# A state-space layer and a GELU layer on one core: the first four chunks of tokens brought in as rows of four, and the order of all steps written as a list

## The chip, the cores and the metric

The kernel runs on one core of a Trainium2 chip. The metric is the device time in microseconds of one execution; three executions of the kernel before were timed, and a fourth execution was profiled. The engines are called PE (TensorE, with its weight loads as PEld), DVE (VectorE), ACT (ScalarE), POOL (GpSimd) and SP (SyncE, which issues nearly all transfers).

## The reference

Four batches of 768 tokens with eight heads pass through a scan with decaying state, and the result through a two-layer network with a tanh GELU. Cut to what matters:

```python
# x: (4, 8, 768, 32)   a: (4, 8, 768)   B, C: (4, 8, 768, 16)
log_a = np.log(np.clip(a, 1e-6, 1.0))
for c in range(S // 32):                      # chunks of the reference
    cum = np.cumsum(la, axis=-1)
    L = np.exp(cum[..., :, None] - cum[..., None, :]) * causal
    y = einsum(C, B) * L @ x  +  (C @ state) * exp(cum)
    state = exp(sum(la)) * state + sum_j B_j x_j exp(cum[-1] - cum_j)
h = y.transpose(0, 2, 1, 3).reshape(3072, 256) @ w_in       # 256 x 2048
out = gelu_tanh(h) @ w_out                                  # 2048 x 256
```

The kernel takes and gives fp32 and multiplies in bf16.

## The kernel before

**Tiling.** The kernel works on chunks of Q = 128 tokens, 24 in all (NCH), six for each batch (CPB). `UNITS` groups them: chunk 0 alone, chunk 1 alone, then eleven pairs. The eight heads lie side by side, so that B and C of a chunk are 128 x 128 (heads times 16 states) and x is 128 x 256.

**Decays.** Instead of exponentials of sums, a scan (`f_R`) multiplies the decays backward from the end of each chunk, `f_RT` and `f_RT0` turn the result to one token per partition with fp32 products, and B is multiplied by it and C by its reciprocal (`f_mul`, `f_mul0`). `f_pe`, `f_pp` and `f_pend` make one decay per chunk, spread over the partitions.

**Attention of a unit.** The scaled B and C are transposed (`f_T`, `f_T0`), evicted (`f_E`, `f_bh0`, `f_ce0`, `f_F`; C twice, masked for even and odd heads), and B is transposed back (`f_N`, `f_bn`). Then, for each unit: `f_G` makes the 128 x 128 products of B and C of all heads, `f_M` masks them to the causal triangle on DVE, `f_D` makes the contribution to the state, `f_S` adds it to the decayed state, `f_SP` spreads the state for the next chunk, `f_Y` adds both parts of y in PSUM, and `f_yev` evicts y, already transposed, to `xm`.

**The two layers.** `f_s1` multiplies a group of the first layer, four products of 128 x 128 weights with 256 tokens, into one of two PSUM buffers (pool `psh`), `f_gelu` evicts it, `f_s2` multiplies four of the 16 parts of the second layer, `f_oev` evicts 128 tokens and `f_store` stores them.

**Weights.** `w_in` and `w_out` come in four pieces each (`load_wi`, `load_wo`, 512 KB) into six buffers and are cast to bf16 (`f_wi`, `f_wo`), mostly on POOL. The cast of `w_in` also reorders the columns, so that columns k, k+4, k+8 and so on of a piece become adjacent, to suit the order in which `w_out` is loaded.

**Loads.** x is loaded one chunk at a time with a token on each partition, which makes pieces of 128 bytes; B and C of chunk 0 likewise, in pieces of 64 bytes; B and C of a batch with six tokens on each partition, in pieces of 384 bytes. All but two go through SP's queue.

**Order.** Every step is a `Node` with an engine, a duration, dependencies, a priority and the buffers that it takes. `run_order` walks through them in time and writes down an order, which is also the order of issue on each engine. Where PE would be idle early on, `idle` puts in products of zeros (77 fillers, L776), which nobody reads.

Of the kernel before, what the change touches and what calls it, by code (L numbers as in the profile page):

```python
# [8 lines left out]
FP32 = mybir.dt.float32  # L9
BF16 = mybir.dt.bfloat16  # L10
AF = mybir.ActivationFunctionType
ALU = mybir.AluOpType

# [17 lines left out]
def run_order(nodes, pools, hop=0.08, same=0.04, idle=None, wait=()):  # L31
# [6 lines left out]
    def est(n):  # L38
        t = 0.0
        for d in n.deps:  # L40
            if d.end is None:
                return None
            t = max(t, d.end + n.after
                    + (d.done + hop if d.eng != n.eng else 0.0 if n.eng == "PE" else same))
        for pool, _ in n.allocs:
            h = hist[pool]
            if len(h) >= pools[pool]:
                for d in h[-pools[pool]]:
                    if d.end is None:
                        return None  # L50
                    t = max(t, d.end + (same if d.eng == n.eng else hop))
        return t
# [41 lines left out]
def kernel(  # L94
# [10 lines left out]
    nc = tc.nc  # L105
# [4 lines left out]
    CPB = S // Q  # L110
    R6 = CPB
    NCH = batch * CPB
    HC = CPB // 2
    HS = S // 2
    d_ff = moe_w_in.shape[1]
# [3 lines left out]
    UNITS = [[0], [1]] + [[c, c + 1] for c in range(2, NCH, 2)]  # L119
    NU = len(UNITS)  # L120

    const = ctx.enter_context(tc.tile_pool(name="const", bufs=1))
    ld = ctx.enter_context(tc.tile_pool(name="ld", bufs=batch))
    wfp = ctx.enter_context(tc.tile_pool(name="wfp", bufs=6))
    ldx = ctx.enter_context(tc.tile_pool(name="ldx", bufs=NU))
# [13 lines left out]

    a_t = const.tile([64, HS], FP32, name="a_t")  # L140
    a_half = [bass.AP(tensor=a.tensor, offset=a.offset + i * HS, ap=[[S, batch * H], [1, HS]])
              for i in range(2)]
    XF, X16 = {}, {}
    U = [dict() for _ in range(batch)]
    bc0 = const.tile([128, 2, H, N], FP32, name="bc0")

    def load_bc0(i, q):
        q.dma_start(out=bc0[:, i], in_=(B, C)[i][0, :, 0:Q, :].rearrange("h p n -> p h n"))

    def load_bc(b, i):  # L150
        d = U[b]
        if "bc" not in d:
# [4 lines left out]
    nc.sync.dma_start(out=a_t[0:32], in_=a_half[0])  # L157
    nc.scalar.dma_start(out=a_t[32:64], in_=a_half[1])
    load_bc0(1, nc.sync)
    load_bc0(0, nc.scalar)  # L160

    wz = const.tile([128, 512], BF16, name="wz")
    nc.vector.memset(wz, 0.0)
    warm = const.tile([128, 1], FP32, name="warm")
    nc.vector.memset(warm, 0.0)  # L165
    nc.scalar.activation(warm, warm, AF.Gelu_apprx_tanh)
    ends = const.tile([64, Q], FP32, name="ends")
    nc.vector.memset(ends, 0.0)
    nc.vector.memset(ends[:, Q - 1:Q], 1.0)
    ac = const.tile([64, HS + 1], FP32, name="ac")  # L170
    nc.vector.memset(ac[:, HS:HS + 1], 0.0)
    pe1 = const.tile([64, HC], FP32, name="pe1")
    pe2 = const.tile([64, 2 * batch, HC], FP32, name="pe2")

    idf = const.tile([64, 64], FP32, name="idf")
    nc.gpsimd.memset(idf, 0.0)
    nc.gpsimd.affine_select(out=idf, in_=idf, pattern=[[-1, 64]], compare_op=ALU.not_equal,
                            fill=1.0, base=0, channel_multiplier=1)
    ident = const.tile([128, 128], BF16, name="ident")
    make_identity(nc, ident)  # L180
    bmask = const.tile([128, H * D], BF16, name="bmask")
    nc.gpsimd.memset(bmask, 1.0)
    bm3 = bmask.rearrange("p (h d) -> p h d", h=H)
    nc.gpsimd.affine_select(out=bm3, in_=bm3, pattern=[[-N, H], [0, D]],
                            compare_op=ALU.is_ge, fill=0.0, base=0, channel_multiplier=1)
    nc.gpsimd.affine_select(out=bm3, in_=bm3, pattern=[[N, H], [0, D]],
                            compare_op=ALU.is_ge, fill=0.0, base=N - 1, channel_multiplier=-1)
    tri = const.tile([128, Q], BF16, name="tri")
    make_upper_triangular(nc, tri, val=1.0, diag=True)
    tri_b = tri.rearrange("p (o q t) -> p o q t", o=1, q=1).to_broadcast([128, 4, 2, Q])  # L190

    sel8 = const.tile([64, H], FP32, name="sel8")
    nc.vector.tensor_reduce(out=sel8, in_=idf.rearrange("p (b h) -> p h b", h=H),
                            op=ALU.add, axis=mybir.AxisListType.X)
    selp = const.tile([64, H, N], FP32, name="selp")
    nc.vector.tensor_copy(out=selp, in_=sel8.rearrange("p (h o) -> p h o", o=1)
                          .to_broadcast([64, H, N]))
    m8 = const.tile([64, 2 * batch], FP32, name="m8")
    nc.gpsimd.memset(m8, 1.0)
    nc.gpsimd.affine_select(out=m8, in_=m8, pattern=[[-H, 2 * batch]], compare_op=ALU.is_ge,  # L200
                            fill=0.0, base=0, channel_multiplier=1)
    nc.gpsimd.affine_select(out=m8, in_=m8, pattern=[[H, 2 * batch]], compare_op=ALU.is_ge,
                            fill=0.0, base=H - 1, channel_multiplier=-1)
    par = const.tile([128, 2], FP32, name="par")
    bmp = bmask.rearrange("p (g e d) -> p e g d", g=4, e=2)
    for e in range(2):
        nc.vector.tensor_reduce(out=par[:, e:e + 1],
                                in_=bmp[:, e, :, 0:1].rearrange("p g o -> p (g o)"),
                                op=ALU.add, axis=mybir.AxisListType.X)
    r_t = const.tile([64, HS], FP32, name="r_t")  # L210

    rt = const.tile([128, R6, batch * H], FP32, name="rt")
    pt = const.tile([128, R6, batch * H], FP32, name="pt")
    q0 = const.tile([128, H], FP32, name="q0")
    bc0s = const.tile([128, 2, H, N], BF16, name="bc0s")
    ce0 = const.tile([128, 2, Q], BF16, name="ce0")
    bh0 = const.tile([128, Q], BF16, name="bh0")
    pend = const.tile([128, NCH], FP32, name="pend")
    WF = {}
    w_in_sb = const.tile([128, 2, d_ff], BF16, name="w_in_sb")  # L220
    w_out_sb = const.tile([128, NF, d_model], BF16, name="w_out_sb")
    xm = const.tile([128, 2, n_tokens], BF16, name="xm")


    gb = ps1.tile([128, 4, 512], FP32, name="gb")
    yb = ps1.tile([128, 512], FP32, name="yb")
    y4 = yb.rearrange("p (c w t) -> p c w t", c=2, w=2)
    rp0 = yb[:, 0:H]
    T6 = [gb[:, 2 * i, 0:S // 2].bitcast(BF16) for i in range(2)]
    T6_0 = [yb[:, 0:S // 2].bitcast(BF16), T6[1]]  # L230

    T0, DT, MT, RP = {}, {}, {}, {}
    state = {}
    gts, ops, hps, outs = {}, {}, {}, {}

    def load_x(u):
        b, c = divmod(UNITS[u][0], CPB)
        XF[u] = ldx.tile([128, 2, H, D], FP32, name="x_t")
        for k in range(len(UNITS[u])):
            nc.sync.dma_start(out=XF[u][:, k], in_=x[b, :, (c + k) * Q:(c + k + 1) * Q, :]  # L240
                              .rearrange("h p d -> p h d"))

# [10 lines left out]

    def copy(eng, o, i):
# [7 lines left out]
    def f_wi(q, k0, k1, eng):  # L262
        for k in range(k0, k1):
            copy(eng, w_in_sb[:, k, q * 512:(q + 1) * 512].rearrange("d (k p) -> d k p", k=4),
                 WF[("i", q)][:, k].rearrange("d (p k) -> d k p", k=4))

    def f_wo(q, eng):
        copy(eng, w_out_sb[:, 4 * q:4 * q + 4], WF[("o", q)])


    def f_clip(i0, i1):
        nc.vector.tensor_scalar(out=ac[:, i0:i1], in0=a_t[:, i0:i1], scalar1=1e-6, scalar2=1.0,
                                op0=ALU.max, op1=ALU.min)
# [7 lines left out]
    def f_RT0():  # L281
        nc.tensor.matmul(out=rp0, lhsT=r_t[0:32, 0:Q], rhs=idf[0:32, 0:H], start=True, stop=True,
                         skip_group_check=True)

    def f_RT(r0, r1):
        if r0 == 0:
            RP[1] = psh.tile([128, 512], FP32, name="hp")[:, 0:R6 * batch * H] \
                .rearrange("p (r j) -> p r j", r=R6)
        r6 = r_t.rearrange("q (p r) -> q r p", r=R6)
        for r in range(r0, r1):  # L290
# [6 lines left out]
    def f_recip0():  # L297
        nc.vector.reciprocal(q0, rp0)

# [3 lines left out]
    def f_recip(b0, b1):  # L303
        js = slice(b0 * H, b1 * H)
        nc.vector.reciprocal(pt[:, :, js], (rt if b0 else RP[1])[:, :, js])
# [17 lines left out]


    def f_mul0(i):
        nc.vector.tensor_tensor(
            out=bc0s[:, i], in0=bc0[:, i],
            in1=(rp0, q0)[i].rearrange("p (h o) -> p h o", o=1).to_broadcast([128, H, N]),
            op=ALU.mult)

    def f_T0(i):
        T0[i] = psh.tile([128, 512], FP32, name="hp").bitcast(BF16)[:, 0:Q]
        nc.tensor.transpose(out=T0[i], in_=bc0s[:, i].rearrange("p h n -> p (h n)"), identity=ident)

    def f_ce0():
        for e in range(2):
            nc.vector.tensor_scalar(out=ce0[:, e], in0=T0[1], scalar1=par[:, e:e + 1],
                                    scalar2=None, op0=ALU.mult)

    def f_bh0():  # L340
# [472 lines left out]
```

## Time and profile before

| | |
|---|---|
| three timed runs | 124.19, 124.71 and 126.72 us, median 124.71 |
| profiled execution | span 122.8 us, 3507 instructions; the page gives no total of its own beside the span |
| PE | 114.6 us busy (93%), 1506 products, of them 77 fillers |
| DVE, ACT, POOL | 68.3, 74.9, 23.0 us busy |
| last product, last eviction, end | PE ends at 119.1, DVE's last eviction takes 0.42 us, the span ends at 122.8 |
| transfers | 14.09 MB in 40591 packets, 35904 of them under 512 bytes |

PE's busy time counts fillers and products at half clock like any other, and products overlap, so a busy PE need not be doing useful work at its full rate. A row of a group reads: line, engine, operation, output and input, sizes, how many; then busy time, mean duration of one, and the idle time of the engine before them. A row of windows reads: the stretch, its length, the busy time of PE, PEld, DVE, ACT and POOL with the number of instructions, the granted clock of PE (1.00 is full), the share of the DMA engines and the GB/s that they moved.

### The profile page before, as it was taken

Reading aid. Unit: us, or ns where it says so; the run is one execution under the profiler, and the core shown is the slowest. Engines: PE = TensorE matmul, PEld = TensorE weight load, DVE = VectorE, ACT = ScalarE, POOL = GpSimd, SP = SyncE. Lnnn points to the kernel's source line nnn. Section 1 sums busy time; section 2 is a strip of 40 time slices with the busy share of each in tenths; the row PEclk is TensorE's granted clock in tenths of the full one; section 3 lists DMA queues with packets and bytes.
Section 4 is the critical chain, followed back from the end, with each engine's and each line's share of the span. In section 5 each row is a group of like instructions: output and inputs, shape, how many; then the busy total and the mean of one; then the engine's idle time right before and its main releaser. Section 6 shows DMA issues by size and latency. Waiting matters only on the chain.

```text
span 122.8 us, 3507 instructions
## 1 busy us (share of the span) xinstructions
PE 114.6 (93%) x1506; PEld 96.2 (78%) x1506; DVE 68.3 (56%) x116; ACT 74.9 (61%) x145; POOL 23.0 (19%) x38
## 2 busy tenths in 40 slices
PE   5899978989799999999999999999999999999970
PEld 5687747778678798787879889787878888888860
DVE  3897999968849888184979672475663000000110
ACT  4025536674676677656686777865768766786310
POOL 7206967750320160122000000000000000000000
PEclk9975699999999999999999999999999999999999
DMA  3999959989799899851101101101110111100121
GB/s 52 242 266 265 328 112 370 320 191 200 128 229 221 127 235 216 145 134 48 43 0 48 43 0 48 43 0 48 43 43 5 45 43 45 45 21 22 43 90 43
DMA packets 40591, 14.09 MB, mean 115 GB/s; under 512 B 35904, under 2 KB 39040, under 8 KB 40576
## 3 DMA queue, kind: packets, MB, share of 16 engines
q1 hardware_dynamic: 39488, 13.75, 46.4%
q8 instruction: 12, 0.20, 0.7%
q10 hardware_dynamic: 1088, 0.11, 0.7%
q14 instruction: 3, 0.02, 0.1%
HBM read 10.72 MB, written 3.15 MB: 113 GB/s over the span
## 4 chain that ended last, share of the span: by engine, by line
PE 70%; SPq 18%; DMA 5%; DVE 3%; issue 1%; DVEq 0%
PE o_ps L523 29%; PE hp L506 29%; SPq L240 7%; DMA bc_t<-in_B_dram 5%; SPq L252 5%; SPq L154 4%; PE yb L523 3%; SPq L248 3%; PE gb L408 2%; PE yb L451 2%; PE yb L460 2%; PE gb L358 2%; DVE ch L260 2%; PE gb L379 1%; DVE bc L349 1%
## 5 line engine op out<-in xcount | busy, mean ns | idle before, releaser
L514 ACT ACTIVATE gT<-hp 128x512 bf16<-128x512 f32 x96 | 53.6, 596 | 24.4 <-PE hp L506 24.2
L506 PE MATMUL hp<-xm,w_in_sb 128*128 128x256 bf16 (+1 forms) x416 | 53.7, 267 | 0.9 <-POOL w_in_sb L258 0.4
L523 PE MATMUL o_ps<-w_out_sb,gT 128*128 128x256 bf16 x352 | 47.3, 273 | 0.0
L506 PEld LDWEIGHTS <-w_in_sb 128*128 128x128 bf16 x416 | 37.6, 99 | 7.7 <-issue 2.0
L523 PEld LDWEIGHTS <-gT 128*128 128x128 bf16 x384 | 37.1, 98 | 4.8 <-issue 0.4
L418 DVE TENSOR_TENSOR m<-gb,tri 128x1024 bf16<-128x1024 f32 (+1 forms) x25 | 29.1, 1173 | 1.9 <-PE gb L408 1.8
L532 DVE COPY o_sb<-o_ps 128x256 f32<-128x256 f32 x2 | 0.8, 424 | 25.6 <-PE o_ps L523 25.6
L258 POOL CAST x<-x_t 128x512 bf16<-128x512 f32 (+1 forms) x12 | 8.5, 710 | 25.0 <-DMA x_t<-in_x_dram 20.1
L479 DVE SCALAR_TENSOR_TENSOR s_new<-s_new,pend,hp 128x64 f32<-128x64 f32 x16 | 4.5, 279 | 11.5 <-PE hp L429 11.2
L776 PE MATMUL o_ps<-wz 128*128 128x128 bf16 x77 | 8.9, 267 | 1.3 <-DVE warm L165 1.3
L530 ACT ACTIVATE o_sb<-o_ps 128x256 f32<-128x256 f32 x20 | 7.7, 385 | 3.8 <-PE o_ps L523 2.1
L486 DVE SCALAR_TENSOR_TENSOR sp_new<-s_new,pend,bmask 128x256 bf16<-128x256 f32 x20 | 10.0, 506 | 0.0
L469 ACT ACTIVATE xm<-yb 128x512 bf16<-128x512 f32 (+1 forms) x13 | 7.3, 564 | 4.3 <-PE yb L460 2.1
L258 POOL CAST w_in_sb<-wf 128x512 bf16<-128x512 f32 x6 | 7.0, 1193 | 7.0 <-DMA wf<-in_moe_w_in_dram 7.0
L776 PEld LDWEIGHTS <-wz 128*128 128x128 bf16 x77 | 6.5, 122 | 1.8 <-DVE warm L165 1.2
L460 PE MATMUL yb<-m,x 128*32 128x128 bf16 x192 | 6.3, 223 | 0.6 <-DVE m L418 0.6
L373 DVE TENSOR_SCALAR ce<-ch,par 128x768 bf16<-128x768 bf16 (+2 forms) x10 | 5.9, 634 | 0.8 <-ACT ch L256 0.8
L451 PE MATMUL yb<-ce,sp_new 128*32 128x128 bf16 x160 | 5.3, 221 | 0.0
L408 PE MATMUL gb<-ce,bh 32*128 32x256 bf16 x96 | 5.1, 278 | 0.0
L460 PEld LDWEIGHTS <-x 128*32 128x32 bf16 x192 | 3.8, 97 | 1.5 <-issue 1.5
L358 PEld LDWEIGHTS <-bc 128*128 128x128 bf16 x48 | 3.8, 110 | 1.3 <-issue 1.1
L258 POOL CAST w_out_sb<-wf 128x1024 bf16<-128x1024 f32 x4 | 4.4, 1112 | 1.5 <-DMA wf<-in_moe_w_out_dram 1.5
(72 smaller groups left out, 61.6 us busy)
## 6 DMA issues: line engine op xcount, KB each, us to landing
x_t<-in_x_dram SPq DMA_DIRECT2D x24, 128.0 KB, 4.5
out_dram<-o_sb SPq DMA_DIRECT2D x24, 128.0 KB, 1.7
wf<-in_moe_w_in_dram SPq DMA_DIRECT2D x4, 512.0 KB, 6.9
wf<-in_moe_w_out_dram SPq DMA_DIRECT2D x4, 512.0 KB, 6.0
bc_t<-in_C_dram SPq DMA_DIRECT2D x4, 384.0 KB, 4.4
bc_t<-in_B_dram SPq DMA_DIRECT2D x4, 384.0 KB, 5.4
bc<-in_B_dram ACTq DMA_DIRECT2D x1, 64.0 KB, 4.2
bc<-in_C_dram SPq DMA_DIRECT2D x1, 64.0 KB, 2.8
```

The lines of the kernel that those rows point to most:

```text
L240: nc.sync.dma_start(out=XF[u][:, k], in_=x[b, :, (c + k) * Q:(c + k + 1) * Q, :] .rearrange("h p d -> p h d"))
L258: nc.gpsimd.tensor_copy(out=o, in_=i)
L408: nc.tensor.matmul(out=gb[:, g, 256 * k:256 * k + 256], lhsT=bh_of(gc)[32 * g:32 * g + 32], rhs=ce_of(gc)[32 * g:32 * g + 32], start=True, ...
L418: nc.vector.tensor_tensor(out=MT[gc][:, g0:g1], in0=gb[:, g0:g1, 256 * k:256 * k + 256] .rearrange("p g (e t) -> p g e t", e=2), in1=tri_b ...
L451: nc.tensor.matmul(out=y4[32 * j:32 * j + 32, k, w], lhsT=sp[:, 32 * h:32 * h + 32], rhs=ce_of(gc)[:, h % 2], start=first(j), stop=False, ...
L460: nc.tensor.matmul(out=y4[32 * j:32 * j + 32, k, w], lhsT=X16[u][:, k, 32 * h:32 * h + 32], rhs=m[:, h // 2, h % 2, :], start=first(j), st ...
L486: nc.vector.scalar_tensor_tensor(out=sp_new.rearrange("p (g d) -> p g d", g=4), in0=state[("s", gc)].rearrange("p (o d) -> p o d", o=1).to ...
L506: nc.tensor.matmul(out=hp[:, j * nt:(j + 1) * nt], lhsT=w_in_sb[:, kc, fi * 128:(fi + 1) * 128], rhs=xm[:, kc, t0:t0 + nt], start=(kc == 0 ...
L514: nc.scalar.activation(gts[u][:, i * per:(i + 1) * per, 0:nt], hps.pop((u, i)).rearrange("p (j t) -> p j t", j=per), AF.Gelu_apprx_tanh)
L523: nc.tensor.matmul(out=ops[gc], lhsT=gts[u][:, fi, tt * Q:(tt + 1) * Q], rhs=w_out_sb[:, fi, :], start=(fi == 0), stop=(fi == NF - 1), ski ...
L530: nc.scalar.activation(o_sb, ops.pop(gc), AF.Copy)
L776: nc.tensor.matmul(out=zb[:, 0:128], lhsT=wz[:, 0:128], rhs=wz[:, 0:128], start=True, stop=True)
```

## The change

1. All twelve units are pairs of chunks.
2. B and C of chunks 0 to 3 are loaded together with four tokens on each partition (pieces of 256 bytes), those of chunks 4 and 5 with two. The decays of batch 0 come in a tile of their own (`a0_t`, 48 rows of 128), those of the other batches are worked out later (`decays`).
3. x of chunks 0 to 3 is loaded as rows of four tokens as well (pieces of 512 bytes). `f_XX` sets it to one token per partition with products by 0/1 matrices (`unp`); `f_XD` makes the state contributions of these four chunks straight from the rows.
4. The first pair's mask goes by quarters: `f_M0` does two of the four groups of heads on DVE, ACT evicts the other two (`f_GE`), and POOL and DVE mask one each (`f_M0s`). Its y is evicted in two halves, and its part of the second layer goes quarter by quarter, both chunks in turn.
5. `w_in` is cast without reordering, one half piece at a time; `f_s1` reads its weight columns four apart (`w_in_k`).
6. The order is a list of node numbers (`ORDERED`; A, D or P after a number moves the step to ACT, DVE or POOL; fN puts in N fillers, 47 in all). Evictions may now go to ACT or DVE.
7. Buffers: seven for weights, two instead of four for B and C of a batch, six for x.

The core of the diff:

```diff
-    UNITS = [[0], [1]] + [[c, c + 1] for c in range(2, NCH, 2)]
-    NU = len(UNITS)
+    NU = NCH // 2
+    GR = ((0, 4), (4, 2))
...
+    def load_bc0(g, i, q=None):
+        c, n = GR[g]
+        (q or nc.sync).dma_start(out=BC0[g][:, i],
+                                 in_=(B, C)[i][0, :, c * Q:(c + n) * Q, :]
+                                 .rearrange("h (p r) n -> p h (r n)", r=n))
...
+    def load_x4():
+        WF["x"] = wfp.tile([128, H, R4 * D], FP32, name="wf")
+        nc.sync.dma_start(out=WF["x"], in_=x[0, :, 0:R4 * Q, :].rearrange("h (p r) d -> p h (r d)", r=R4))
...
-    def f_wi(q, k0, k1, eng):
-        for k in range(k0, k1):
-            copy(eng, w_in_sb[:, k, q * 512:(q + 1) * 512].rearrange("d (k p) -> d k p", k=4),
-                 WF[("i", q)][:, k].rearrange("d (p k) -> d k p", k=4))
+    def f_wi(q, k, eng):
+        copy(eng, w_in_sb[:, k, q * 512:(q + 1) * 512], WF[("i", q)][:, k])
...
+    def f_RT0(g):
+        c0, n = GR[g]
+        m = Q // n
+        rr = r0_t.rearrange("q (p r) -> q r p", r=n)
+        for r in range(n):
+            for c in range(n):
+                nc.tensor.matmul(out=rp0[g][m * c:m * c + m, r], lhsT=rr[:, r],
+                                 rhs=id0[:, :, c0 + c], start=True, stop=True,
+                                 tile_position=(0, m * c), skip_group_check=True)
...
+    def f_XX(u):
+        for r in range(R4):
+            for k in range(2):
+                c = 2 * u + k
+                cs = slice(P4 * c, P4 * c + P4)
+                nc.tensor.matmul(out=XN[c][:, 0:H * D], lhsT=unp[cs, r].rearrange("p q s -> p (q s)"),
+                                 rhs=x4b[cs, :, r], start=(r == 0), stop=(r == R4 - 1),
+                                 tile_position=(P4 * c, 0), skip_group_check=True)
+
+    def f_XD(u):
...
+        for r in range(R4):
+            for g in range(4):
+                for k in range(2):
...
+                    nc.tensor.matmul(out=XN[c][32 * g:32 * g + 32, H * D:H * D + 64],
+                                     lhsT=bc0s[0][cs, 0, r, 2 * g:2 * g + 2].rearrange("p h n -> p (h n)"),
+                                     rhs=x4b[cs, 2 * g:2 * g + 2, r], start=(r == 0), stop=(r == R4 - 1),
+                                     tile_position=(P4 * c, 32 * g), skip_group_check=True)
...
     def f_s1(u, i):
...
+            q, k = divmod(2 * i + j, 4)
+            for w in range(2):
+                nc.tensor.matmul(out=hp[:, j * T:(j + 1) * T], lhsT=w_in_k[:, w, q, k],
+                                 rhs=xm[:, w, u * T:(u + 1) * T], start=(w == 0), stop=(w == 1))
...
-    for t, fn in run_order(nodes, pools, idle=idle, wait=("DVE", "POOL")):
-        fn()
+    for w in ORDERED.split():
+        if w[0] == "f":
+            fill(int(w[1:]))
+        else:
+            n = nodes[int(w.rstrip("ADP"))]
+            n.eng = {"A": "ACT", "D": "DVE", "P": "POOL"}.get(w[-1], n.eng)
+            n.fn()
```

In the new order PE runs, after the opening fillers: f_RT0 for both groups of chunks, the transposes of C and B of chunks 0 to 3, G of unit 0, f_pp0, XD(0), XX(0), G(1), Y(0), XD(1), XX(1), then the first s1 groups of unit 0 with Y(1), the first group of the second layer and the transposes of chunks 4 and 5 among them. SP issues the first `w_in` pieces after x, then the first `w_out` piece, the last `w_in` piece, B and C of chunks 4 and 5, the other `w_out` pieces, B and C of batch 1 and then x of the later pairs.

## The prediction

> **What bounds the kernel now.** I read the page first (slices, chain), then TensorE (PE) stage by stage, then its groups. The profiled execution has a span of 122.8 us; the three timed runs have a median of 124.71 us, so 1.9 us lie outside the span, and I keep them unchanged. On this kernel a measurement tells about 2% from no change: the cut for "faster" is 122.2 us.
>
> ```profile
> PEclk9975699999999999999999999999999999999999
> DMA  3999959989799899851101101101110111100121
> GB/s 52 242 266 265 328 112 370 320 191 200 128 229 221 127 235 216 145 134 48 43 0 48 43 0 48 43 0 48 43 43 5 45 43 45 45 21 22 43 90 43
> ...
> PE 70%; SPq 18%; DMA 5%; DVE 3%; issue 1%; DVEq 0%
> ```
>
> The chain ends on PE, and its first quarter is the SP queue and a load: two stages. DMA is full until about 40 us and nearly idle afterwards. The stages, from the table of windows:
>
> ```profile
> 0.00:13.60 13.60, 11.78 (x122) 9.52 (x123) 10.01 (x31) 4.78 (x12) 6.41 (x20) 0.79 0.91 223
> 13.60:31.74 18.14, 15.71 (x257) 12.40 (x258) 16.21 (x22) 10.68 (x20) 10.25 (x11) 0.97 0.95 238
> 31.74:119.10 87.36, 87.09 (x1128) 74.25 (x1127) 41.64 (x65) 59.43 (x115) 6.30 (x9) 1.00 0.33 76
> 119.10:122.80 3.70, 0.00 (x0) 0.00 (x0) 0.42 (x1) 0.00 (x0) 0.00 (x0) 1.00 0.11 39
> ```
>
> From 31.74 to 119.10 PE is busy 87.09 of 87.36 us: there only its work counts. The last 3.70 us are the last eviction and store. All that can be won lies before 31.74, where "busy" includes 77 filler products and stretches at half clock. The groups of the dense stage:
>
> ```profile
> L523 PE MATMUL o_ps<-w_out_sb,gT 128*128 128x256 bf16 x328 | 43.8, 273 | 0.0
> L506 PE MATMUL hp<-xm,w_in_sb 128*128 128x256 bf16 x324 | 43.8, 273 | 0.0
> ...
> L523 PE MATMUL yb<-w_out_sb,gT 128*128 128x256 bf16 x32 | 4.0, 273 | 0.0
> ```
>
> and two lines of the timeline that give the rate (starts 0.87 us apart for 8, so 0.109 us each; the 273 ns include the drain):
>
> ```profile
> 37.93 1.04 PE L506 MATMUL hp<-xm,w_in_sb 128*128 128x256 bf16 x8
> 38.80 1.04 PE L523 MATMUL o_ps<-w_out_sb,gT 128*128 128x256 bf16 x8
> ```
>
> So the dense stage holds 684 big products, 74.6 us, and 12.7 us of attention.
>
> **The change, part by part.** The question is when the first product of the first layer (s1) starts, what PE must do from there, and what it loses.
>
> *Work from the first s1 on.* All twelve units are now pairs, so 768 big products remain: 84 more than in the dense stage, 84 x 0.109 = 9.2 us. Two more Y (0.56 each) and one D and G (0.4 with the change-over) make 1.6; 12 more transposes at 0.056 are 0.7; the decay products of the other batches (f_RT, f_pp), which move behind the opening, cost 1.6 (L293's row below) and 0.5 (L316, 0.62 at half clock). Sum: 87.4 + 9.2 + 1.6 + 0.7 + 1.6 + 0.5 = 101.0 us. In these terms the kernel before has PE end at 119.1 = 101.0 + 18.1: it behaves as if it had started the dense work at 18.1 us.
>
> *The opening.* Rows for it:
>
> ```profile
> 4.05 0.41 PEld L282 LDWEIGHTS yb<-idf,r_t 32*128 32x128 f32 x2 [0.33 <-POOL m L200]
> ...
> 6.60 1.57 PE L293 MATMUL hp<-idf,r_t 32*64 32x32 f32 x24
> ...
> 19.87 0.49 PEld L506 LDWEIGHTS <-w_in_sb 128*128 128x128 bf16 x8
> ```
>
> Log decays of batch 0 land at 2.9 (issue 0.80, landing 2.0 to 2.1); VectorE (DVE) has more constants to make and is free at 3.5. Clip 0.2 and scan 0.42 end at 4.15. f_RT0 is 16 fp32 products, two passes each, 32 columns wide: L293's passes, 64 wide, start 0.057 apart (1.3 us over 23), so 32 passes cost 0.96 us by width and 1.8 us if 0.057 is a floor; I take 1.2 with the latency, for the passes above scale with width (0.14 apart at 128 columns). It ends at 5.4. The reciprocal (208 ns for 8 columns, 457 for 48) is 0.35; two multiplies at 512 columns (291 ns at 128, 957 at 768) are 0.69 each: 7.15. Four transposes of B 0.4, eviction on DVE 0.4 (275 ns at 128), eight G products 0.6 at half clock (four took 0.40): 8.55. f_pp0 0.62, then XD(0), 32 small products, 0.5, and XX(0), 8 products of 256 columns in two row groups, 1.05 at half clock (four pairs of 0.213 and the drain): 10.75. Two ScalarE (ACT) evictions of 0.385: 11.5. Y(0), 24 products, 0.75 (8 took 0.41 at half clock): 12.25. XD(1) and XX(1) stand ahead of s1 on PE, 1.35 more: **13.6 us**. Beside it and not last: the mask (M0 1.22, ready 9.8; f_SP 0.51; the quarters through ACT, DVE and POOL by 10.9), the two xm evictions (13.0), and the x load: 1.07 MB go to its end, which the page's slices give at 6.7 us, its casts end at 8.6 (DVE's half stands after the B eviction), and XD(0) comes at 9.2. Without that cover each us late is a us on the path. If PE had full clock throughout and the constants cost nothing, 12.0; if f_RT0 is at the floor and the row groups don't overlap in XX (0.9 each time), 16.3.
>
> *Losses after the first s1.* Gelu takes 596 ns per group of four products against 0.437 on PE, with two PSUM buffers, so the first eight groups run at ACT's pace: 8 x 0.16 = 1.3. The half clock:
>
> ```profile
> 7.75:8.00 0.25, 0.25 (x8) 0.52 0.87 238
> ...
> 14.50:14.75 0.25, 0.16 (x3) 0.83 1.40 320
> ```
>
> Here it lasted from 7.8 to 14.5; with the same end, 0.9 us of s1 run at half rate, 0.5 lost. Together 1.8; at least 0.8 (the second layer's groups filling the pace), at most 3.5 (half clock for twice as long). Up to the last gelu of unit 1 ACT has 14.2 us of work and PE some 15.5, so neither starves the other for long. [...] The change issues 47 fillers, not 77. [...]
>
> *Loads.* Weight pieces are cast unstrided, about 0.6 us for 512 columns (x casts: 613) where the strided ones took 1193: POOL is earlier, worth nothing as long as loads set its pace. On DVE yev(1), and on PE the groups s1(0,6) onward, are queued behind B and C of chunks 4 and 5; 3.9 MB end with C, by the page's slices at 18.4 us, and PE comes there at about 19. Chunks 4 and 5 of x end 6.7 MB, 28.0 us and a cast of 0.6, and D(2) stands at 31. Both are hidden, with 0.6 and 2.4 us of cover; a us beyond it is a us lost. The x of unit 5 ends 8.5 MB, 37.8 us, for a product at about 41.
>
> *Weights read with a stride.* s1's weight columns now stand four apart. Loads with 128 adjacent columns start at most 0.056 apart (L506 above) and hide under 0.109. The nearest strided row, r_t in L293, is 0.057 for 64 columns, 0.114 for 128: 5 ns over, x 384 = 1.9 us. Two passes of 128 fp32 columns (L282) are 0.14 apart: 12 us. I take nothing, since the stride is the only difference from the L506 row, and keep 12 us for a rival. [...]
>
> *The sum.* 13.6 + 101.0 + 1.8 = 116.4 for the end of PE, against 119.1: 2.7 us less. The tail is unchanged, so span 120.1 and 124.71 - 2.7 = **122.0 us**. The bounds I believe together (12.6 with 1.0; 14.3 with 2.4) give 120.2 to 123.3.
>
> **The rivals.** *A, the opening keeps full clock.* For it: the page has full clock until 7.8, and the fillers stand between the steps. Against it: in the row at 7.75 above the clock fell at a time when fillers and small products had kept PE busy for most of the three us before. First s1 at 12.0, loss 0.8: 113.8, 5.3 us less, 119.4 us.
>
> *B, the front gives it back.* For it: twice the data per step, 16 small fp32 products where one stood. At the upper bound, 16.0 and 2.0, PE ends at 119.0: 124.6 us, no change.
>
> *C, the strided weight load is the bound.* Its place is the loads of s1 in all twelve units. For it: in the dense stage the load windows already fill 74.25 of 87.36 us beside the products. It decides from 2.7 / 384 = 7 ns over 0.109, that is 0.116 us a load; at L282's 0.14 the sum is 122.0 + 12 = 134 us, slower. Against it: bf16 and the full width, as now.
>
> **How the numbers follow.** Forecast 0.50, A 0.30, B 0.10, C 0.10. The forecast's own range has the 122.2 cut a little above its middle: 0.3 of its 0.5 is faster by over 2%, 0.2 is within. A is all faster, B 0.08 within and 0.02 slower, C slower. So faster 0.60, same 0.28, slower 0.12. The range goes from under A, 118.2, to just over B, 125.0; C is left out.
>
> **What would show it.** Right: the first s1 product (line 702 of the changed kernel) at 13 to 14.5 us, PE idle under 2.5 us from there to its end, rate 0.109 in the dense stage, big products beginning in earnest near 14 instead of 20. Wrong: its loads more than 0.116 apart; PE waiting on DMA between 17 and 32; half clock to 18; f_RT0 (line 367) taking over 2 us; gaps in the dense stage, where a fixed list of steps puts a product behind a late DVE or ACT step.

## The result, and the profile after

The changed kernel takes **125.84 us** (median of 20 runs, 124.90 to 126.69) beside 124.85 us for the kernel before on the same chip (20 runs, 124.16 to 126.72): a ratio of 1.0072, interval 1.0046 to 1.0098. Forecast were 122.0 us, with 118.2 to 125.0 as the range. So it is a little slower, by less than 2%. Ratios leave disturbed runs out, and where the runs of a kernel below lie in two groups they keep only the lower one, so for such a kernel I compare medians of all its runs.

The page of after, in the places that were shown of before:

```profile
PEclk9999869999999999999999999999999999999999
DMA  3999999995395996951101101110111011102111
...
PE 80%; ACT 6%; DVE 4%; issue 4%; POOL 2%; POOLq 0%; DVEq 0%
```

Two things did come as intended. The loads are off the chain of work that ended last (18% SP queue and 5% DMA before, none now), and DMA is busy up to about the same slice as before. In their place the chain has ACT and DVE. The windows, cut at the first s1 product and at the end of PE:

```profile
0.00:15.70 15.70, 11.34 (x218) 8.88 (x218) 9.89 (x33) 6.25 (x15) 8.08 (x25) 0.96 0.92 265
15.70:31.74 16.04, 15.42 (x174) 12.95 (x173) 13.89 (x25) 12.13 (x24) 5.53 (x9) 0.93 0.85 217
31.74:119.60 87.86, 86.99 (x1154) 77.56 (x1153) 47.38 (x81) 55.57 (x105) 4.49 (x6) 1.00 0.29 70
119.60:123.30 3.70, 0.00 (x0) 0.00 (x0) 0.00 (x0) 0.38 (x1) 0.00 (x0) 1.00 0.11 37
```

The tail is 3.70 us as before. The first s1 product comes at 15.70 us (forecast 13.6), and from there PE needs 103.9 us to its end (forecast 102.8). Both parts are over, and together they are the 3.2 us between the forecast end of PE, 116.4, and 119.6. The execution of this profile took 124.97 us, 0.87 under the median, so the profile accounts for 3.2 of the 3.84 us between 125.84 and the forecast. First the opening, in the timeline of after (start, duration, engine, line; in brackets how long the engine was idle and whom it waited for):

```profile
4.09 1.20 PE L367 MATMUL yb<-idf,r_t 48*32 48x8 f32 x40 [0.40 <-POOL m L274]
...
6.34 0.68 DVE L442 TENSOR_TENSOR bc0s<-bcf,yb 128x512 bf16<-128x512 f32 x1
...
7.08 1.12 PE L991 MATMUL yb<-wz 128*128 128x128 bf16 x9 [1.78 <-DVE bc0s L442]
7.99 0.63 PE L451 MATMUL hp<-ident,bc0s 128*128 128x128 bf16 x4
...
10.70 0.60 ACT L620 ACTIVATE ge<-gb 128x512 bf16<-128x512 f32 x1
11.40 1.22 DVE L606 TENSOR_TENSOR m<-gb,tri 128x1024 bf16<-128x1024 f32 x1 [1.09 <-ACT ge L620]
12.66 0.60 ACT L620 ACTIVATE ge<-gb 128x512 bf16<-128x512 f32 x1 [1.18 <-DVE m L606]
```

What to see: the third and fourth rows, and the last three. PE stands still for 1.78 us ahead of **fillers**, products that nobody reads: they write to `yb`, where the decays lie that DVE's multiply (second row) is reading until 7.02. The transposes of C, whose input has been ready since 6.42, are queued behind them and start at 7.99. Then ACT and DVE, which were to do the mask's quarters beside each other, take turns: the first copy, the mask of two quarters, the second copy, each waiting for the one before although they read different banks of `gb`. (L620 and L606 are the lines of `f_GE` and `f_M0`.)

Second the stage behind, in what PE waited for from the first s1 on, and one place of it in the timeline:

```profile
PE gb L497 <- DVE ch L343: 0.6, 1, 0.6
PE gb L497 <- ACT ch L339: 0.5, 1, 0.5
PE gb L590 <- DVE bh L343: 0.2, 1, 0.2
```

```profile
67.47 0.50 PE L497 MATMUL gb<-ident,bc 128*128 128x128 bf16 x6
67.80 0.60 PE L702 MATMUL hp<-xm,w_in_sb 128*128 128x256 bf16 x4
69.02 0.49 PE L497 MATMUL gb<-ident,bc 128*128 128x128 bf16 x6 [0.61 <-DVE ch L343]
```

```profile
68.01 0.95 DVE L343 COPY ch<-gb 128x768 bf16<-128x768 bf16 x1
```

L497 is `f_T`, the transposes of a batch's C (67.47) and B (69.02). They go to different banks of `gb`, and yet B's wait until DVE's eviction of C has ended at 68.96. With four products 0.109 us apart the row at 67.80 would have been done at 68.24, so 0.78 us are lost: 0.61 of idle time, and 0.17 in which PE only drains but counts as busy. Over the whole stage PE is idle for 1.49 us (0.62 and 0.87 in the windows above).

Last the clock, as the profile records it, and two products of XX(0), which have 256 columns:

```profile
14.00:14.50 0.50, 0.50 (x45) 0.40 (x51) 0.46 (x3) 0.33 (x2) 0.50 (x2) 0.91 1.16 215
14.50:17.50 3.00, 3.00 (x49) 1.81 (x44) 2.21 (x5) 1.63 (x4) 2.15 (x4) 0.50 0.90 239
17.50:18.00 0.50, 0.50 (x5) 0.36 (x4) 0.50 (x1) 0.37 (x1) 0.00 (x0) 0.68 0.84 311
```

```profile
11.44 0.28 PE L555 MATMUL o_ps<-x4b,unp 32*128 32x256 bf16 x1
11.55 0.27 PE L555 MATMUL o_ps<-x4b,unp 32*128 32x256 bf16 x1
```

By the record the clock falls to half at 14.41 us and is back at 17.82; the s1 products run at half rate until then, not until 14.5. Before about 11 us the products show half rate too, though the record says 1.00 there: eight products of G(0) take 0.61 us from 10.04, those of G(1) 0.40 from 13.30. Between the two PE had full clock, with XX(0) 0.11 us apart.

### The profile page after: what moved, and what is told of

Its sections match the earlier page's. It is cut to its first block, busy times and chain, and to the rows that moved or that the text cites. A ratio compares the mean times of both kernels' runs of the same rounds, so it can differ in the third digit from the quotient of the medians.

```text
span 123.3 us, 3607 instructions
## 1 busy us (share of the span) xinstructions
PE 113.7 (92%) x1543; PEld 99.4 (81%) x1543; DVE 71.2 (58%) x138; ACT 74.3 (60%) x144; POOL 18.1 (15%) x39
## 4 chain that ended last, share of the span: by engine, by line
PE 80%; ACT 6%; DVE 4%; issue 4%; POOL 2%; POOLq 0%; DVEq 0%
PE hp L702 33%; PE o_ps L720 29%; PE gb L590 3%; PE yb L660 3%; PE yb L651 3%; PE yb L720 2%; ACT ce L464 2%; PE gb L497 2%; DVE ch L343 1%; ACT gT L706 1%; PE hp L407 1%; PE yb L991 1%; PE gb L516 1%; DVE m L606 1%; PE yb L367 1%
## 5 line engine op out<-in xcount | busy, mean ns | idle before, releaser
L702 PE MATMUL hp<-xm,w_in_sb 128*128 128x256 bf16 x384 | 54.6, 277 | 0.1
L702 PEld LDWEIGHTS <-w_in_sb 128*128 128x128 bf16 x384 | 41.4, 114 | 3.7 <-issue 1.7
L597 DVE TENSOR_TENSOR m<-gb,tri 128x1024 bf16<-128x1024 f32 x22 | 26.2, 1216 | 0.2 <-PE gb L590 0.2
L343 DVE COPY o_sb<-o_ps 128x256 f32<-128x256 f32 x8 | 3.4, 424 | 12.8 <-PE o_ps L720 10.7
L341 POOL CAST x<-x_t 128x512 bf16<-128x512 f32 x9 | 6.5, 732 | 27.2 <-DMA x_t<-in_x_dram 15.7
L991 PE MATMUL yb<-wz 128*128 128x128 bf16 x47 | 6.0, 299 | 2.8 <-DVE bc0s L442 1.8
L339 ACT ACTIVATE xm<-yb 128x512 bf16<-128x512 f32 (+1 forms) x8 | 4.2, 544 | 0.6 <-PE hp L629 0.4
L341 POOL CAST w_in_sb<-wf 128x512 bf16<-128x512 f32 x7 | 4.2, 637 | 0.0
L651 PEld LDWEIGHTS <-sp_new 128*32 128x32 bf16 x160 | 2.9, 96 | 1.4 <-issue 1.2
L720 PE MATMUL yb<-w_out_sb,gT 128*128 128x256 bf16 x32 | 4.0, 272 | 0.0
```

Source lines behind the costliest of these rows:

```text
L339: nc.scalar.activation(o, i, AF.Copy)
L341: nc.gpsimd.tensor_copy(out=o, in_=i)
L343: nc.vector.tensor_copy(out=o, in_=i)
L597: nc.vector.tensor_tensor(out=MT[gc].rearrange("p g e t -> p (g e) t"), in0=gb[:, :, 256 * k:256 * k + 256] .rearrange("p g (e t) -> p g e ...
L651: nc.tensor.matmul(out=y4[32 * j:32 * j + 32, k, w], lhsT=sp[:, 32 * h:32 * h + 32], rhs=ce_of(gc)[:, h % 2], start=first(j), stop=False, ...
L702: nc.tensor.matmul(out=hp[:, j * T:(j + 1) * T], lhsT=w_in_k[:, w, q, k], rhs=xm[:, w, u * T:(u + 1) * T], start=(w == 0), stop=(w == 1))
```

## The experiments

**Theory 1:** the fillers, put into `yb` by the change, hold up the opening. **Theory 2:** two engines that read one PSUM tile, and a product that writes one bank while another is read, take turns, because the program orders them by tile. **Theory 3:** the half clock has its share. Rivals: the strided weight load (C of the prediction), and the order as a list.

**The fillers in their own bank.** Until the first G they go to a bank of `gb`:

```diff
-            nc.tensor.matmul(out=yb[:, 256:384], lhsT=wz, rhs=wz, ...
+            nc.tensor.matmul(out=yb[:, 256:384] if filled[0] else gb[:, 3, 0:128], lhsT=wz, rhs=wz, ...
```

> The changed kernel with the fillers that stand ahead of the first G written into a bank of gb, which nobody reads yet, instead of yb, which holds the turned decays that DVE is still reading. Theory 1 (nine fillers wait for DVE's second multiply in yb, and the transposes of C stand behind them): the transposes of C start at about 6.5 us instead of 7.99, the first s1 product at about 14.3 instead of 15.7, the time falls by 1.0 to 1.5 us, to 124.3 to 124.8 (ratio to before 0.995 to 1.000). Rival 1 (the opening is set by the chain of ACT and DVE evictions, and the fillers' wait was covered): first s1 at 15.4 or later, time within 0.3 us of 125.8 (ratio 1.005 or more).

Measured: 124.32 us, ratio to the kernel before 0.9965 (0.993 to 1.0). Timeline of PE:

```profile
5.23 1.14 PE L994 MATMUL gb<-wz 128*128 128x128 bf16 x9
6.49 0.61 PE L451 MATMUL hp<-ident,bc0s 128*128 128x128 bf16 x4
...
8.51 0.61 PE L591 MATMUL gb<-ce,bh 32*128 32x256 bf16 x8
```

The nine fillers run at 5.23 with no wait, the transposes of C start at 6.49, 1.50 us earlier, and the first s1 product comes at 14.83 in place of 15.70. That is only 0.87 us earlier because this execution had half clock throughout the opening (XX(0) 0.21 us apart) and that of after had not. The run with adjacent columns below has the opening of after, and in its profile that ran at half clock as well (XX(0) 0.21 us apart): there s1 comes at 16.36, so the whole 1.5 us carry through. Against the kernel before, the changed kernel goes from 1.0072 to 0.9965: 1.1%, or 1.3 us. Theory 1 holds: without this wait the change is level with the kernel before or just under it, with it just over.

**No fillers at that place.** The same wait, taken away otherwise:

```diff
-... 57 51 52 f9 59 62 ...
+... 57 51 52 59 62 ...
```

> The changed kernel without the nine fillers between f_RT0 and the transposes of C, all else as it is (the later fillers still write yb). Theory 1: the transposes of C start at about 6.5 us, as with the other bank; the three fillers behind them then wait in yb instead, until DVE's second multiply ends at 7.0, which the transposes of B wait for anyway; first s1 at 14.3 to 14.6, 1.0 to 1.4 us less than 125.8. Rival 1: no change beyond 0.3 us. Rival 2 (the fillers earn the clock): the clock at full later than in the changed kernel, time longer than 125.8.

Measured: 124.70 us, ratio 0.9972 (0.9948 to 0.9996); the transposes start at 6.49 and s1 at 14.84. The nine fillers were worth nothing and cost 0.9 us of the opening.

**Adjacent weight columns.** s1 reads 128 adjacent columns of `w_in` where the change reads every fourth; the casts stay as they are, so the hidden units come in another order and the output is not the reference's:

```diff
-                nc.tensor.matmul(out=hp[...], lhsT=w_in_k[:, w, q, k],
+                nc.tensor.matmul(out=hp[...], lhsT=w_in_sb[:, w, (2 * i + j) * 128:(2 * i + j + 1) * 128],
```

> The changed kernel with s1's weights read as 128 adjacent columns instead of columns four apart; the casts are left as they are, so the hidden units come in another order than the second layer's rows and the output is not the reference's. Rival C of the prediction (the strided load is dearer): the time falls by 0.5 us or more, products of s1 under 0.109 us apart or fewer gaps. My theory: the load's record shortens from 114 to 98 ns, the starts stay 0.109 us apart, and the time stays within 0.3 us of 125.8.

Measured: 125.51 us, ratio 1.0029 (0.9999 to 1.006). The group of loads in after, and then in this run (the middle figures are busy us and mean ns of one):

```profile
L702 PEld LDWEIGHTS <-w_in_sb 128*128 128x128 bf16 x384 | 41.4, 114 | 3.7 <-issue 1.7 <-POOL w_out_sb L341 0.4
```

```profile
L702 PEld LDWEIGHTS <-w_in_sb 128*128 128x128 bf16 x384 | 36.9, 99 | 6.9 <-issue 1.6 <-POOL w_in_sb L341 0.4
```

The stride lengthens a load from 99 to 114 ns on the mean, but in the dense stage eight products take 0.87 us from start to start in both (47.08 to 47.95 in after, 47.53 to 48.41 here). The loads hide; rival C falls.

**Unit 0's mask on DVE, first try.** The run with the own bank, the quarters given up for two masks of a chunk each, and the spread of the state put between them:

```diff
     def f_M0():
+        f_M(0, 0)
+        if ("sp", 0) not in state:
+            nodes[80].fn()          # f_SP(0)
+        f_M(0, 1)
+        return
...
-75 74 6 69 70 55 76 80 77 72 f3 ...
+75 6 69 55 74 70 76 77 72 f3 ...
```

> The filler bank of the first kernel, and the mask of the first pair undone: DVE alone masks all quarters in two instructions with f_SP(0) between them; no ACT eviction of G and no POOL quarter. Theory 2 (two engines that read the same PSUM tile are put one after another, so the quarters of ACT and DVE take turns, 0.60 + 1.22 + 0.60 us, and cost as much as DVE alone): Y(0) no later than with the filler bank alone, first s1 0.2 to 0.6 us earlier, time 0.2 to 0.6 us less than that kernel's. Rival (the quarters run beside each other once the front is early): first s1 0.5 us later or more and the time 0.5 us longer than that kernel's.

Measured: 124.77 us, ratio 0.9992 (0.996 to 1.0025), s1 at 15.38. A miss of mine, and again the same kind of wait:

```profile
10.39 0.48 DVE L692 SCALAR_TENSOR_TENSOR sp_new<-o_ps,pend,bmask 128x256 bf16<-128x256 f32 x1
...
10.93 0.37 PE L555 MATMUL o_ps<-x4b,unp 32*128 32x256 bf16 x1 [0.72 <-DVE sp_new L692]
```

`f_SP(0)` now stood ahead of `f_XX(0)` in the order and reads the tile into which XX writes, so XX waited for it.

**Unit 0's mask on DVE, second try.** Both masks ahead of `f_SP(0)`, that behind XX again:

```diff
     def f_M0():
+        f_M(0, 0)
+        return
...
     def f_M0s(g, eng):
+        if g == 3:
+            f_M(0, 1)
+        return
...
-... 76 80 77 72 f3 90 78 8 71 ...
+... 76 78 80 77 72 f3 90 8 71 ...
```

> As the run with the fillers in their own bank, but unit 0's mask is two whole-chunk instructions on VectorE (1.22 us each), with nothing on ScalarE and GpSimd. Theory 2 (the quarters take turns, so the split buys nothing): VectorE masks from 9.2 to 11.65, Y(0) at 12.2 against 12.76 because ScalarE copies x half a us earlier, and the median is no worse than 124.3 (123.8 to 124.5). Rival (the quarters do save VectorE time that matters): Y(0) after 13, median 124.8 or more.

Measured: 124.24 us, ratio 0.9957 (0.9926 to 0.9988), Y(0) at 12.25 against 12.76 (in a profiled execution of 126.08 us). Some 0.2 us of this are the clock: G(0) ran at full rate here, 0.40 us against 0.61. One engine alone does in two instructions what three engines did in five with turns, and not later.

**Two gram tiles.** `gb` becomes two tiles of two banks each; the masks of the later units are then two instructions:

```diff
-    gb = ps1.tile([128, 4, 512], FP32, name="gb")
+    ga = ps1.tile([128, 2, 512], FP32, name="ga")
+    gc_ = ps1.tile([128, 2, 512], FP32, name="gc")
...
-    T6 = [gb[:, 2 * i, 0:S // 2].bitcast(BF16) for i in range(2)]
+    T6 = [G2[i][:, 0, 0:S // 2].bitcast(BF16) for i in range(2)]
...
     def f_M(u, k):
+        for h in range(2):      # one mask for each tile
```

> The gram buffer gb (four banks, one tile) is declared as two tiles of two banks; fillers stay out of yb as in the run with their own bank; every mask of units 1 to 11 becomes two half-size instructions, which adds a few us to VectorE where it idles. Theory 2 (two engines that read one PSUM tile take turns because the program orders them by tile): ScalarE's copies of quarters 2 and 3 start with VectorE's mask of quarters 0 and 1 (both within 0.1 us of the end of G(0)) instead of ahead and behind it, G(1) comes about 1.2 us earlier, Y(0) starts at about 12.0 in place of 12.76, and the median falls by 0.4 to 0.8 us against the run with the own bank (124.3): about 123.7. Rival (the turns come from the PSUM itself, the engines cannot read it together): the instructions lie beside each other but each takes longer, and Y(0) stays at 12.7; or they still take turns.

Measured: 122.26 us (119.72 to 123.20, six runs) beside 124.75 for the kernel before, and measured again:

> The run with two gram tiles once more, beside its variant and the kernel before with two tiles, since its six runs lay at 119.8 and at 122.4: median 122.0 to 122.6, some runs near 119.8.

122.38 us (119.98 to 123.05, six runs) beside 124.44. Nine of the twelve runs lie at 122.15 to 123.2, three at 119.7 to 120.0; these have no trace, and their cause is open. The first ratio, 0.9603 (0.9538 to 0.9668), stands for such runs alone, so I go by the medians: 2.0 us under the kernel with one gram tile (124.24 in the run above and 124.19 in one below, measured beside the same kernel before), 2.1 to 2.5 under the kernel before. This is far more than I expected. The opening, in the timeline:

```profile
9.21 0.60 ACT L624 ACTIVATE ge<-gc 128x512 bf16<-128x512 f32 x1
9.24 1.23 DVE L610 TENSOR_TENSOR m<-ga,tri 128x1024 bf16<-128x1024 f32 x1 [0.44 <-PE gc L593]
```

Copy and mask start together and take 0.60 and 1.23 us, where in after they took 0.60 and 1.22 one after the other: the PSUM served both, and the turns were the program's. But s1 comes only 0.23 us earlier, at 14.60, since G(1) stands behind XX on PE and uses little of it. The rest was won where I had not looked, in the dense stage:

```profile
65.15 0.50 PE L499 MATMUL gc<-ident,bc 128*128 128x128 bf16 x6
65.48 0.60 PE L706 MATMUL hp<-xm,w_in_sb 128*128 128x256 bf16 x4
65.92 0.50 PE L499 MATMUL ga<-ident,bc 128*128 128x128 bf16 x6
```

B's transposes follow at 65.92 with no wait, while DVE still evicts C (65.69 to 66.64). The windows from the first s1 to the end of PE, in this kernel and in after:

```profile
14.60:116.49 101.89, 101.80 (x1328) 90.62 (x1326) 62.19 (x126) 67.89 (x128) 11.48 (x16) 1.00 0.40 97
```

```profile
15.70:119.60 103.90, 102.41 (x1328) 90.51 (x1326) 61.27 (x105) 67.70 (x128) 10.02 (x15) 0.99 0.38 93
```

The same 1328 products take 2.01 us less: 1.40 of idle time are gone, and 0.61 that had counted as busy. Put beside each other, the two timelines draw apart at four places, each at products that write `gb`: by 0.31 us at the second pair's G (23.61 in after), 0.63 and 0.78 at transposes of B (31.84 and 69.02) and 0.32 at the transposes back of B (52.43), together 2.04. From the first s1 to Y(1) the two need the same, 3.72 and 3.75 us, so the clock has no part in the gain; and none of the four places waits for a mask, so the halved masks have none either. Theory 2 holds, and is worth more behind the opening than in it.

**Two gram tiles in the kernel before**, the same edit:

> The kernel before with its gram buffer as two tiles of two banks, nothing else: masks of two halves each. Theory 2 in the dense stage: the kernel before also made TensorE wait for VectorE at the gram buffer (1.4 us at two lines), so it gains 0.5 to 1.5 us: 123.2 to 124.3. If the two tiles gain as much here as in the changed kernel (2.4 us, to about 122.3), their gain has nothing to do with this change; if they gain nothing, it was the changed opening that needed them.

Measured: 123.75 us beside 124.44, ratio 0.9952 (0.9916 to 0.9987). The kernel before has the same tile, but gains 0.7 us, not 2.0: after 13 us its waits at `gb` go from 0.8 to 0.2 us, but those for the casts of `w_in` (L506, here L509) go from 0.6 to 1.2. So it had less to win at this tile, 0.8 us of waits against some 1.4, and most of what two tiles bring belongs to the changed kernel.

**The planner's own order.** The same nodes without the list:

```diff
-    if not ORDERED:
+    if True:                    # run_order writes the order
...
-    for w in ORDERED.split():
+    for w in ():
```

> The changed kernel with the order that the planner finds by itself from the same nodes, not the written list. If the list is what loses the time, this is faster than 125.8 by 1 us or more; if the opening's waits lose it (the planner's fillers write to yb as well, its quarters read one tile as well), it stays at 125.5 or is slower, up to 128, with the same wait of the first fillers for VectorE.

Measured: 127.81 us (four runs, 126.59, 126.79, 128.83 and 128.90), ratio 1.019 (1.0128 to 1.0251). Timeline and waits:

```profile
6.84 0.91 PE L991 MATMUL yb<-wz 128*128 128x128 bf16 x7 [1.00 <-DVE bc0s L442]
```

```profile
PE hp L702 <- ACT gT L706: 0.5, 2, 0.2
PE hp L629 <- ACT bn L339: 0.3, 1, 0.3
PE o_ps L720 <- ACT o_sb L339: 0.3, 1, 0.3
PE gb L516 <- DVE bh L343: 0.2, 1, 0.2
```

The fillers wait here as well, and s1 starts at 15.73. By the ratios (1.019, of the two shorter runs, against 1.0072) the list is worth about 1.5 us, and more by the medians; as a whole it isn't what loses, but the two long waits at L497 are its own, since this order has none of them.

**The clock, twice.** Four more early fillers close the idle 0.4 us ahead of the decays:

```diff
-... 2 53 f23 49 ...
+... 2 53 f27 49 ...
```

> As the run with the fillers in their own bank, but 27 instead of 23 early fillers, which closes the idle 0.41 us before the decays' transposes. Theory 3 (the clock opens after a stretch of TensorE work without a gap; in the kernel before it opened at about 4.1): fillers at 5.2 come 0.06 us apart instead of 0.12, the opening is shorter by some tenths, and the median moves by -0.3 to 0 us against 124.3. [...]

Measured: 124.19 us, ratio 0.9964 (0.9925 to 1.0003), beside 0.9965 without them. The nine fillers at 5.22 take 1.14 us as before: the gap was not what kept the clock down. Then, XX(1) put behind the first s1 group, and seven products of full size where s1 waits for its input:

```diff
-... 72 f3 90 78 8 71 79 33 31 f3 83 81 91 86 37 84 87 7 85A 35 88 230
+... 72 f5 90 78 8 71 79 33 31 f4 83 81 91 37 84 7 85A 35 h7 230 86 87 88
...
+        if w[0] == "h":        # products of zeros in a buffer of s1
```

> As the run with the fillers in their own bank, but the copy of unit 1's x to tokens (narrow 32-row passes, 1.2 us) moves behind the first s1 product, whose wait is filled with 7 full-size products in another bank, and the two filler groups before Y(0) get 2 and 1 more. Theory 3 (narrow passes keep the clock down: with full-size products from 13.6 on the clock opens at about 14.3 and not at 17.7): s1 products from 14.8 are 0.11 us apart instead of 0.21, and the median falls by 1 to 1.5 us to about 123. [...]

Measured: 124.87 us, ratio 1.0052 (1.0012 to 1.0092). Windows, and the timeline of PE:

```profile
14.00:15.50 1.50, 1.50 (x41) 0.88 (x41) 0.00 (x0) 0.14 (x1) 0.61 (x1) 0.50 0.57 104
15.50:17.00 1.50, 0.71 (x10) 0.48 (x11) 0.36 (x2) 0.87 (x2) 1.17 (x2) 0.98 0.64 183
```

```profile
16.87 1.03 PE L703 MATMUL hp<-xm,w_in_sb 128*128 128x256 bf16 x8 [0.79 <-DVE s_new L678]
```

The clock opened at 15.5, but the early clock went into a wait: s1's next buffer is the one that XX(1) took, and it comes free only when `f_S` has read it. Whether the fuller products opened the clock, one profile can't say: here it also fell to half some 2 us earlier than in after, before those products, since G(1) still ran at full rate (0.40 us from 11.76) and Y(0) at half (0.43 us for eight products from 12.79, 0.31 in after). It was back at 15.5, 2.3 us earlier than in after (17.82). Theory 3 stays open.

**Both causes removed as far as I could.** Two gram tiles; C's transposes evicted by ACT alone and B's by DVE alone; no fillers just ahead of Y(0):

```diff
-... 59 62 61 f3 60 5 65 63D 66 f5 73 ...
+... 59 62 61A f3 60 5 65 63D 66D f5 73 ...
...
-79 33 31 f3 83 81
+79 33 31 83 81
```

> As the run with two gram tiles; besides, C's transposes of the first four chunks are evicted by ScalarE alone and B's by VectorE alone, so that no two engines read one tile, and the three fillers just before Y(0) go. Theory 2: G(0) starts at 8.3 in place of 8.52, Y(0) at 12.0 in place of 12.52, the first s1 product at 14.0 to 14.2 in place of 14.60, and the median falls by 0.2 to 0.6 us against the same two tiles run beside it. Rival (the half clock, which opens at its own time near 17.7, takes back what is begun earlier): s1 starts earlier but the median stays within 0.2 us.

Measured: **121.97 us** (120.23 to 122.48, six runs) beside 124.44, ratio 0.9759 (0.9698 to 0.982). In the timeline:

```profile
7.12 1.57 ACT L466 ACTIVATE ce<-hp,par 128x256 bf16<-128x256 bf16 x4 [1.21 <-PE hp L453]
...
7.87 0.75 DVE L345 COPY bh<-hp 128x256 bf16<-128x256 bf16 x2 [0.85 <-PE hp L453]
...
14.15 1.04 PE L706 MATMUL hp<-xm,w_in_sb 128*128 128x256 bf16 x4
```

ACT and DVE now evict side by side, from different tiles; Y(0) starts at 12.08 and s1 at 14.15, 0.45 us earlier than with two tiles alone. The median falls by 0.4, about all of it, but within what six runs scatter. This version lies under both kernels by its median; the interval leaves open whether it is faster than the kernel before by more than 2%.

## Why the prediction was wrong

**Wrong: the first s1 product at 13.6.** It came at 15.70. By the steps: f_RT0 took 1.20 us as taken (with the second group's four products, which the sum had not counted), the multiplies 0.69 and 0.68, and B's scaled half was done at 7.02 (7.15 in the sum). The step "Four transposes of B 0.4, eviction on DVE 0.4 (275 ns at 128), eight G products 0.6" failed: its G products were to start at 7.95 and started at 10.04. The sum put no fillers ahead of the transposes, though the list has nine there, and they write to `yb`, where those of the kernel before wrote to `o_ps`; without that wait G starts at 8.51 (shown), 1.53 us earlier. Of the other 0.56, two engines taking turns at the evictions are 0.16, since with one engine for each tile G starts at 8.35. The rest lies in the step itself: there the transposes of B start at 7.20 and their eviction at 7.87, 0.67 us where the sum had 0.40, and G follows 0.48 later.

"Beside it and not last: the mask ... by 10.9" failed by the turns at `gb`: from G to Y(0) the forecast had 3.55 us, with turns it is 4.25 (8.51 to 12.76, the fillers in their own bank), with two tiles, divided evictions and no fillers 3.73 (8.35 to 12.08). From Y(0) to s1, 2.1 were forecast and 2.07 taken in both. Both runs had half clock there (XX(1) 0.21 us apart in both), as the sum assumed. In the profile of after G to s1 took 5.66 us, where the sum had 5.65, but that is luck: full clock from about 11 to 14.4 us made up for the turns. With the same opening at half clock, in the run with adjacent columns, it took 6.32.

**Wrong by an absent term: the losses behind.** Between its first s1 product and its first product of Y(1), at 19.42, the changed kernel lost 3.72 - 20 x 0.109 = 1.5 us to half clock and gelu pace, which the sum had at 1.8. That it came so near is luck as well: the half clock cost (17.82 - 15.70) / 2 = 1.06 instead of 0.5, and so gelu pace only 0.5 instead of 1.3. What the sum did not have were the waits at `gb`: 1.40 us of idle time and the drains around four of them, together 2.0 by what two tiles took away. The trace of before has such waits at its own `gb` (0.8 us at L358), and the sum did not carry them over:

```profile
31.74 0.49 PE L358 MATMUL gb<-ident,bc 128*128 128x128 bf16 x6 [0.62 <-DVE ch L260]
```

The larger one ends at 31.74, just where the sum lets its dense stage begin, so that "there only its work counts" left it out. The dense stage's work itself is 103.9 - 1.5 - 2.0 = 100.4 us, where the sum had 101.0 (in it, two Y of 0.56 and 0.4 for D and G make 1.5, not 1.6).

**The balance of PE's end:** 2.1 (opening) - 0.3 (half clock and pace) + 2.0 (waits at `gb`) - 0.6 (work) = 3.2 us over 116.4. With most of these waits taken away the kernel takes 121.97 us, close to the forecast: in its profile s1 comes 0.55 us later than forecast, and from there to the end of PE it needs 102.14 us instead of 102.8. So the sum was a good account of the work, and a bad one of who waits for whom.

**The clock** was at half until 17.82 in s1, where the sum had 14.5; "half clock to 18" was among the signs of a wrong forecast. By the record it had been at half for 3.41 us, and no run shows what began or ended that. What opened it at about 11 us in after (XX(0) 0.11 us apart), and not in the run with adjacent columns, which has the same opening (0.21), stays open.

**The rivals.** A, full clock in the opening, came only in part, from about 11 to 14.4 us. Before that nine fillers take from 7.08 to 7.99, 0.10 us each for 128 columns, while at full clock 256 columns take 0.109. A's ground, that the page of before has full clock until 7.8, does not hold either, since the record gives full clock (1.00 from 1.76 to 3.99 and from 4.49 to 5.05) where the products do not run at one rate:

```profile
1.76 2.23 PE L776 MATMUL o_ps<-wz 128*128 128x128 bf16 x19
...
4.49 0.56 PE L776 MATMUL o_ps<-wz 128*128 128x128 bf16 x7
```

The first 19 fillers start 0.11 us apart, the seven at 4.49 only 0.06. B's time, 124.6, was the nearest, but its reason (small fp32 products at a floor) was not the one. C fell to the run with adjacent columns. **Right:** f_RT0, the multiplies, the rate of 0.109, the hidden loads (no wait of PE for DMA behind the first s1 product), the strided load hidden, the tail. And among the signs of a wrong forecast, "gaps in the dense stage, where a fixed list of steps puts a product behind a late DVE or ACT step" is what L497 shows.

## What to carry to other kernels

Ask of every instruction that is moved to another buffer, even one that nobody needs, who else uses that tile at that time, and what is queued behind it: nine idle products cost 1.3 us here because they were put into a tile that another engine was reading. Where two engines are to work side by side, or one bank is to be filled while another is read, give them tiles of their own; splitting one PSUM tile of four banks in two brought 2.0 us, although it added instructions. When a sum of work is right and the time is not, list the waits of the slow kernel one by one, before looking for a dearer operation.

## What the runs showed of the hardware

- ACT and DVE read different banks of PSUM at the same time at no cost: 0.60 and 1.23 us side by side with two gram tiles, 0.60 and 1.22 one after the other in after.
- A weight load of 128 bf16 columns four apart shows as 114 ns (after) in place of 99 (adjacent columns), and the products stay 0.109 us apart in both.
- The clock fell to half at 14.41 in after, though PE had been busy for 2.0 of the 3.0 us before.
- The record of the granted clock can be wrong: in the run with the own bank it has 1.00 from 14.83 to 17.83, while 16 s1 products take 3.26 us, 0.2 each.
